# Score banks in a fixed round, VectorE's pair work spread over a slot, and the first pair prepared ahead of a branch, in a fused attention and MLP kernel

## The chip, the cores and the metric

One core of one Trainium2 chip runs the whole program. The metric is device time in microseconds (us) of one execution; smaller is better.

TensorE, VectorE (DVE in the profile), ScalarE (ACT), GpSimd (POOL) and SyncE (SP) work side by side on their own queues. PE is TensorE's matmuls, PEld its weight loads.

## The reference

```python
def rmsnorm(x, g):
    return x / np.sqrt(np.mean(x * x, axis=-1, keepdims=True) + 1e-06) * g
# q, k, v: 8 batches, 12 heads, 448 rows, 64 columns (float32)
q_n, k_n = rmsnorm(q, g_q), rmsnorm(k, g_k)
scores = q_n @ k_n.T / sqrt(64)                  # per batch and head
attn = softmax(scores)                           # (max subtraction cut here)
x = (attn @ v) as rows of 768                    # 3584 rows
h = x @ w_in                                     # 768 by 2048, float64 input
out = (h - np.tanh(h)) @ w_out                   # 2048 by 768, float64 input
```

## The kernel before

The program takes two heads at a time: 8 batches of 6 pairs make 48 steps. It has a software pipeline with one *slot* per step. In slot `s` TensorE computes the scores of pair `s+1`, the sums ("totals") and values of pair `s`, and turns (transposes) the normalised rows of pair `s+2`; between these it runs stretches of the MLP of the batch before, by `run(gap)`. Slots 0 to 5 have attention only, and the first pieces of weights. Slots 6 to 11 carry the MLP of the first batch. From slot 12 on the other batches follow in a regular round; this is the steady stage.

The MLP's weights come as float64 words. They are rounded to float32 once, early: ScalarE (`round_weight_a`, L71 and L72), then VectorE (L78, L79, L82), then GpSimd (L90). Three raw buffers go round, and SyncE refills one when it is free. Most of this falls in slots 6 to 11, inside `run(gap)`.

```python
    ps_s = pool("ps_s", bufs=5, space=PSUM)      # five PSUM banks for attention
    ps_m = pool("ps_m", bufs=3, space=PSUM)      # three for products
    def sc_bank():
        return ps_s.tile([P, 512], F32, name="sc")

    def scores(s, c):                            # 64x448 scores of key block c, both heads
        ...                                      # c == KF: the short last block, "p_last"
        tiles = [sc_bank() for _ in range(2)]    # one bank for each head
        ...                                      # matmuls, then per head:
            nc.scalar.activation(p[...], tiles[h][:, :n], AF.Exp, scale=rr[...])

    def slot(s):
        gap = gap_ns(s)
        if s < 2 * NP:                           # NP = 6 pairs of a batch
            totals(s, sc_bank())                 # ends with VectorE's reciprocal
        if has(s + 1):
            scores(s + 1, 0)
            scores(s + 1, 1)
        ...
        run(gap)                                 # MLP products, weight rounding
        if has(s + 2):
            turn(s + 2, sc_bank(), sc_bank())    # ScalarE copies kT and qT out
        ...                                      # squares(s + 3), loads
        run(gap)
        if has(s + 1):
            scores(s + 1, KF)
        ...
        av = [sc_bank() for _ in range(2)]       # the two values banks
        last_values(s, av)
        ...
        divide(s, values(s, av))                 # VectorE: xT = av * reciprocal
        if has(s + 1):
            scores(s + 1, 2)                     # "the second score" below
            add(s + 1)                           # VectorE: sums of exponentials
        if has(s + 3):
            norm(s + 3)                          # VectorE sums, GpSimd power
        run(gap)
        if has(s + 3):
            norm_q(s + 3)                        # VectorE: query rows times power
        run(gap)
```

Before all this, gain vectors are loaded, a flag is worked out from them (it chooses between a path without a row maximum and a general path), and all loads of `q`, `k`, `v` stand behind the branch on that flag.

## Time and profile before

| kernel before | |
|---|---|
| time, median of 3 runs | 1478.01 us (1473.65 to 1478.78) |
| span of the profiled run | 1474.3 us |
| TensorE busy | 1434.7 us, 97% |
| VectorE busy | 809.9 us, 55% |
| first scores; turn in slot 1 | 13.88 us; 37.20 us |
| a slot of the steady stage | 28.94 us, in some slots more |

TensorE bounds the kernel, and the 97% is an average over three stages. The lines that show them (windows, TensorE's waits, two timelines and the chain of waits) stand in the prediction below. Read there which engine is most loaded in which stage: the DMA engines in the opening (from 10 us on), VectorE in the first batch (slots 6 to 11, about 80 to 320 us), and TensorE alone from 320 us on.

This is ScalarE's timeline of the kernel before in slot 8 (start, length, engine, line, operation, output<-input, and in brackets the idle time before it with who ended it):

```profile
176.49 0.91 ACT L71 ACTIVATE w_out<-w_raw 128x768 f32<-128x768 f32 x1 [5.09 <-DMA w_raw<-in_moe_w_out_dram]
177.31 0.89 ACT L72 ACTIVATE w_raw<-w_raw 128x768 int32<-128x768 uint32 x1
178.09 0.77 ACT L422 ACTIVATE p_last<-sc,rr 128x224 f32<-128x224 f32 x2
```

And this is TensorE at the same place, in the same kernel:

```profile
173.42 1.02 PE L417 MATMUL sc<-qT,kT 64*128 64x448 f32 x2
179.53 1.83 PE L417 MATMUL sc<-qT,kT 64*128 64x448 f32 x2 [5.10 <-DVE xT L498]
```

TensorE waits 5.10 us and the profile names VectorE's division (xT, L498), whose signal came at 179.4. But ScalarE's exponential `p_last`, which frees two other banks of the same five, ended at 178.86, only half a microsecond before. It stood in ScalarE's queue behind a weight piece whose transfer had not landed. Nothing asks for those two banks at this moment, so the late exponential has no wait line.

### The profile page before, as it was taken

To read this page: it belongs to the slowest core of one execution; us is meant where nothing else is said; L and a number is where in the kernel's file an instruction comes from. 1 tells how busy PE (TensorE), PEld (TensorE's weight loads), DVE (VectorE), ACT (ScalarE), POOL (GpSimd) and SP (SyncE) were. 2 spreads that over 40 slices of the span, in tenths; PEclk is the share of its full clock that TensorE was granted. 3 is DMA by queue.
4 is the path that set the end of the run, shared out by engine and by line. 5 is a ranking of instruction groups with operands and counts; after the bars stand their busy time and mean duration, and the time that the engine had idled before them with its cause. 6 is when DMAs were issued, how large, how long until landed. Compare 5 with 4: busy or idle time off the path is not lost.

```text
span 1474.3 us, 26066 instructions
## 1 busy us (share of the span) xinstructions
PE 1434.7 (97%) x10272; PEld 1186.9 (81%) x10272; DVE 809.9 (55%) x1245; ACT 455.3 (31%) x850; POOL 508.5 (34%) x378
## 2 busy tenths in 40 slices
PE   6989899999999999999999999999999999999997
PEld 2558664488888888888888888888888888899997
DVE  3997888755554565347535654555555366433322
ACT  5754553133212332223322233213322233200100
POOL 4655656323331334213422233232333133312310
PEclk9999999999999999999999999999999999999999
DMA  8767787864556544654555555546555654455563
GB/s 177 171 190 201 244 252 204 230 186 148 167 145 175 174 143 144 187 166 149 185 141 169 151 163 162 163 138 182 154 167 142 167 183 135 148 166 157 187 191 97
DMA packets 268055, 250.74 MB, mean 170 GB/s; under 512 B 164884, under 2 KB 210196, under 8 KB 267924
## 3 DMA queue, kind: packets, MB, share of 16 engines
q1 hardware_dynamic: 267600, 248.97, 58.0%
q8 instruction: 84, 1.38, 0.4%
q14 instruction: 47, 0.39, 0.1%
q10 hardware_dynamic: 324, 0.00, 0.0%
HBM read 215.48 MB, written 33.42 MB: 169 GB/s over the span
## 4 chain that ended last, share of the span: by engine, by line
PE 89%; DVE 5%; DMA 2%; SPq 2%; ACT 1%; issue 1%; POOL 0%; ACTq 0%; DVEq 0%; POOLq 0%
PE mm L553 64%; PE sc L417 9%; PE sc L464 6%; PE mm L718 5%; PE sc L485 2%; PE sc L452 1%; PE sc L390 1%; PE sc L394 1%; SPq L182 1%; DVE rs L490 1%; SPq L230 1%; DVE xT L498 1%; PE mm L464 0%; DVE w_out L78 0%; DMA gT<-in_moe_w_in_dram 0%
## 5 line engine op out<-in xcount | busy, mean ns | idle before, releaser
L553 PE MATMUL mm<-xT,w_f 128*128 128x224 f32 x1392 | 280.8, 355 | 4.6 <-DVE s L619 4.6
L553 PEld LDWEIGHTS mm<-xT,w_f 128*128 128x128 f32 x1392 | 259.3, 190 | 25.5 <-issue 9.8
L553 PEld LDWEIGHTS mm<-gT,w_f 128*128 128x128 f32 x1344 | 251.4, 190 | 22.5 <-issue 11.4
L553 PE MATMUL mm<-gT,w_f 128*128 128x224 f32 x1344 | 267.7, 355 | 0.0
L373 POOL TENSOR_TENSOR rr<-rr,neg_half 112x8 f32<-112x8 f32 x96 | 157.9, 1666 | 314.3 <-DVE rr L372 314.2
L553 PE MATMUL mm<-tt,w_f 128*128 128x224 f32 x1044 | 211.2, 354 | 0.0
L553 PEld LDWEIGHTS mm<-tt,w_f 128*128 128x128 f32 x1044 | 196.1, 190 | 7.8 <-issue 7.8
L553 PE MATMUL mm<-tg,w_f 128*128 128x224 f32 x1008 | 200.4, 353 | 0.0
L553 PEld LDWEIGHTS mm<-tg,w_f 128*128 128x128 f32 x1008 | 189.5, 190 | 0.0
L417 PE MATMUL sc<-qT,kT 64*128 64x448 f32 (+1 forms) x960 | 172.9, 498 | 12.8 <-DVE xT L498 7.8
L422 ACT ACTIVATE p<-sc,rr 128x448 f32<-128x448 f32 x192 | 106.1, 637 | 200.2 <-PE sc L417 200.2
L590 POOL TENSOR_TENSOR gT<-s,th 128x448 f32<-128x448 f32 x96 | 112.8, 1182 | 153.6 <-ACT th L589 153.6
L513 POOL TENSOR_TENSOR tt<-xT,tt 128x224 f32<-128x224 f32 x23 | 32.4, 1409 | 335.5 <-DVE xT L498 335.5
L417 PEld LDWEIGHTS sc<-qT,kT 64*128 64x128 f32 (+1 forms) x960 | 62.4, 166 | 82.2 <-issue 70.1
L490 DVE RECIPROCAL rs<-sc 128x224 f32<-128x224 f32 x42 | 65.4, 1557 | 77.6 <-PE sc L485 77.5
L422 ACT ACTIVATE p_full<-sc,rr 128x448 f32<-128x448 f32 x96 | 56.0, 632 | 150.1 <-PE sc L417 150.1
L589 ACT ACTIVATE th<-s 128x448 f32<-128x448 f32 x96 | 55.4, 577 | 120.8 <-DVE s L619 63.4
L672 DVE TENSOR_TENSOR s<-mm,s 128x224 f32<-128x224 f32 x21 | 8.2, 392 | 141.8 <-PE mm L553 141.8
L464 PE MATMUL sc<-p,v_nat 128*32 128x224 f32 x1344 | 79.1, 353 | 0.0
L718 PE MATMUL mm<-gT,w_out 128*128 128x448 f32 x192 | 76.0, 552 | 0.0
L422 ACT ACTIVATE p_last<-sc,rr 128x224 f32<-128x224 f32 x96 | 37.9, 448 | 114.9 <-PE sc L417 114.9
L498 DVE TENSOR_TENSOR xT<-sc,rs 64x224 f32<-64x224 f32 x168 | 65.3, 389 | 9.7 <-PE sc L464 2.3
(118 smaller groups left out, 1623.6 us busy)
## 6 DMA issues: line engine op xcount, KB each, us to landing
w_f<-w_in SPq DMA_DIRECT2D x196, 384.0 KB, 3.4
w_f<-w_out SPq DMA_DIRECT2D x147, 512.0 KB, 3.9
w_raw<-in_moe_w_out_dram SPq DMA_DIRECT2D x16, 768.0 KB, 5.1
q_nat<-in_q_dram SPq DMA_DIRECT2D x48, 224.0 KB, 4.6
out_dram<-th SPq DMA_DIRECT2D x192, 56.0 KB, 2.2
k_nat<-in_k_dram SPq DMA_DIRECT2D x96, 96.0 KB, 3.8
v_nat<-in_v_dram SPq DMA_DIRECT2D x48, 192.0 KB, 3.8
w_in<-w_out SPq DMA_DIRECT2D x21, 384.0 KB, 6.0
```

The source lines that it names most:

```text
L373: nc.gpsimd.tensor_tensor(out=r, in0=r, in1=neg_half[:rows], op=ALU.pow)
L417: nc.tensor.matmul(tiles[h][i * keys : (i + 1) * keys, :n], lhsT=kT[r, c * P : c * P + keys], rhs=qT[r, i * n : (i + 1) * n], start=True, ...
L422: nc.scalar.activation(p[:, h, c if c < 2 else 0, :], tiles[h][:, :n], AF.Exp, scale=rr[:, 0, 2 * c + h : 2 * c + h + 1])
L464: nc.tensor.matmul(av[n][r : r + BL, :HS], lhsT=v_nat[:, h, c, m * BL : (m + 1) * BL], rhs=p[c][:, h, n * HS : (n + 1) * HS], start=False, ...
L485: nc.tensor.matmul(dn[r : r + BL, :HS], lhsT=by[n], rhs=moving[2 * n + h], start=(i == 0), stop=(i == len(parts) - 1),)
L490: nc.vector.reciprocal(rs, dn[:, :HS])
L498: nc.vector.tensor_tensor(out=x[m * D : (m + 1) * D, n * HS : (n + 1) * HS], in0=av[n][m * D : (m + 1) * D, :HS], in1=rs[n * D : (n + 1) * ...
L513: eng.tensor_tensor(out=t2, in0=x22, in1=t1, op=ALU.subtract)
L553: nc.tensor.matmul(bank[:, f * HS : (f + 1) * HS], lhsT=w[:, c * width + f, :], rhs=moving[p](c), start=(first and f == 0 and c == 0), sto ...
L589: nc.scalar.activation(th, h, AF.Tanh, bias=0.0, scale=1.0)
L590: eng.tensor_tensor(out=g[:, rows, cols], in0=h, in1=th, op=ALU.subtract)
L718: nc.tensor.matmul(bank[:, :S], lhsT=w_out_row(f, n // HC)[:, n % HC * P : (n % HC + 1) * P], rhs=g[:, f, :], start=(f == 0), stop=(f == C ...
```

## The change

The intent has three parts. (a) The loads, squares, sums and powers of the first pair go ahead of the branch, so that they need not wait for the flag. (b) The banks are handed out in a fixed round, so that the second score no longer draws a bank that VectorE's division must free. (c) VectorE's work for coming pairs, which stood in one block, is spread over four places of a slot. The diff, cut to its core:

```diff
+    with tc.manual_schedule(), tc.tile_pool(name="g", bufs=1) as gp:   # ahead of the branch
+        nc.scalar.dma_start(out=grow[:, 0, :], in_=g_q[None, :])
+        nc.scalar.dma_start(out=grow[:, 1, :], in_=g_k[None, :])
+        for name, src in (("q", q), ("k", k)):
+            fetch(nc, name, early[name], src[0, 0:2])
+        for i, src in enumerate((g_q, g_k)):
+            nc.sync.dma_start(out=gcol[:, i : i + 1], in_=src[:, None])
+        nc.scalar.activation(warm, warm, AF.Exp)
 ...                                              # constants, flag
+        squares_of(nc, early["sq"], early["n"], early["q"], early["k"])
+        norm_of(nc, early["rr"], early["sq"], early["n"], neg_half)
     bounded = nc.values_load(flag[0:1, 0:1])
 ...
-    ps_s = pool("ps_s", bufs=5, space=PSUM)
-    ps_m = pool("ps_m", bufs=3, space=PSUM)
+    ps = pool("ps", bufs=1, space=PSUM)
+    banks = {name: [ps.tile([P, 512], F32, name=f"{name}{i}") for i in range(n)] for name, n in (("sc", 5), ("mm", 3))}
+    turns = {"sc": 0, "mm": 0}
+    def bank_of(name):
+        turns[name] += 1
+        return banks[name][turns[name] % len(banks[name])]
     def sc_bank():
-        return ps_s.tile([P, 512], F32, name="sc")
+        return bank_of("sc")
 ...
             scores(s + 1, 2)
-            add(s + 1)
-        if has(s + 3):
-            norm(s + 3)
-        run(gap)
-        if has(s + 3):
-            norm_q(s + 3)
-        run(gap)
+        for work, n in ((add, 1), (add_last, 1), (norm, 3), (norm_q, 3)):
+            run(gap / 2)
+            if has(s + n):
+                work(s + n)
```

Cut away: `add` is split in `add` and `add_last`; `sq`, `n`, one sum tile and the first pair's rows become fixed tiles; the gain column is made after the first `norm_q`; the general path has smaller buffers.

More of the change, by code (lines that the diff above doesn't have):

```diff
@@ L90, in round_weight_c, with fetch, squares_of, norm_of @@
     nc.gpsimd.tensor_tensor(out=bits, in0=bits, in1=raw[:, :, 0], op=ALU.add)
-def bounded_path(tc, ctx, q, k, v, moe_w_in, moe_w_out, out, g_col, ident, ones, half_ones, neg_half):
+def fetch(nc, name, t, pair):
+    S = pair.shape[1]
+    P = 128
+    KF, KR = S // P, S % P
+    if name == "q":
+        nc.sync.dma_start(
+            out=t.rearrange("p h c d -> p h (c d)"), in_=pair.rearrange("h (p c) d -> p h (c d)", c=NCH)
+        )
+        return
+    full, rest = pair[:, : KF * P].rearrange("h (p c) d -> h p c d", c=KF), pair[:, KF * P :]
+    if name == "v":
+        last = t[:, :, KF]
+        nc.sync.dma_start(
+            out=t[:, :, :KF].rearrange("p h c d -> p h (c d)"), in_=full.rearrange("h p c d -> p h (c d)")
+        )
+    else:
+        last = t[:, KF]
+        for h in range(2):
+            nc.sync.dma_start(out=t[:, :KF, h], in_=full[h])
+    for r in range(2):
+        nc.sync.dma_start(out=last[r * KR : (r + 1) * KR], in_=rest.rearrange("h p d -> p h d"))
+def squares_of(nc, sq, n, q, k):
+    nc.scalar.activation(n.rearrange("p c h d -> p (c h) d"), q.rearrange("p a b d -> p (a b) d"), AF.Square)
+    nc.scalar.activation(sq, k.rearrange("p a b d -> p (a b) d"), AF.Square)
+def norm_of(nc, rr, sq, n, neg_half):
+    D = sq.shape[2]
+    for i, x in ((1, n.rearrange("p c h d -> p (c h) d")), (0, sq)):
+        rows = x.shape[0]
+        r = rr[:rows, i]
+        nc.vector.reduce_sum(r, x, axis=AX.X)
+        nc.vector.tensor_scalar(out=r, in0=r, scalar1=1.0 / D, scalar2=1e-6, op0=ALU.mult, op1=ALU.add)
+        nc.gpsimd.tensor_tensor(out=r, in0=r, in1=neg_half[:rows], op=ALU.pow)
+def bounded_path(tc, ctx, q, k, v, moe_w_in, moe_w_out, out, g_col, ident, ones, half_ones, neg_half, early):
     nc = tc.nc
@@ L148, in bounded_path @@
     wp = wp_stack.enter_context(tc.tile_pool(name="wp", bufs=1))
-    ps_s = pool("ps_s", bufs=5, space=PSUM)
-    ps_m = pool("ps_m", bufs=3, space=PSUM)
+    ps = pool("ps", bufs=1, space=PSUM)
[4 more added lines that the diff above has]
+        return banks[name][turns[name] % len(banks[name])]
     def mm_bank():
-        return ps_m.tile([P, 512], F32, name="mm")
+        return bank_of("mm")
     loaded = {}
@@ L160, in load @@
             src = {"q": q, "k": k, "v": v}[name]
-            bufs = 3 if name == "v" else 2
-            pair = src[b, 2 * hp : 2 * hp + 2]
-            if name == "q":
-                t = nat.tile([CP, 2, NCH, D], F32, name="q_nat", bufs=bufs)
-                nc.sync.dma_start(
-                    out=t.rearrange("p h c d -> p h (c d)"), in_=pair.rearrange("h (p c) d -> p h (c d)", c=NCH)
-                )
-            else:
-                full, rest = pair[:, :K0].rearrange("h (p c) d -> h p c d", c=KF), pair[:, K0:]
-                if name == "v":
-                    t = nat.tile([P, 2, NCH, D], F32, name="v_nat", bufs=bufs)
-                    last = t[:, :, KF]
-                    nc.sync.dma_start(
-                        out=t[:, :, :KF].rearrange("p h c d -> p h (c d)"), in_=full.rearrange("h p c d -> p h (c d)")
-                    )
-                else:
-                    t = nat.tile([P, NCH, 2, D], F32, name="k_nat", bufs=bufs)
-                    last = t[:, KF]
-                    for h in range(2):
-                        nc.sync.dma_start(out=t[:, :KF, h], in_=full[h])
-                for r in range(2):
-                    nc.sync.dma_start(out=last[r * KR : (r + 1) * KR], in_=rest.rearrange("h p d -> p h d"))
+            if s == 0 and name != "v":
+                t = early[name]
+            else:
+                shape = [CP, 2, NCH, D] if name == "q" else [P, NCH, 2, D] if name == "k" else [P, 2, NCH, D]
+                t = nat.tile(shape, F32, name=f"{name}_nat", bufs=3 if name == "v" else 2)
+                fetch(nc, name, t, src[b, 2 * hp : 2 * hp + 2])
             loaded[name, s] = t
@@ L358, in squares @@
     def squares(s):
-        n = nat.tile([CP, NCH, 2, D], F32, name="n", bufs=1)
-        sq = nat.tile([P, 2 * NCH, D], F32, name="sq", bufs=1), n.rearrange("p c h d -> p (c h) d")
-        normed[s] = sq, n
-        for i, name in ((1, "q"), (0, "k")):
-            nc.scalar.activation(sq[i], loaded[name, s].rearrange("p a b d -> p (a b) d"), AF.Square)
-    def norm(s):
-        sq, n = normed[s]
-        rr = small.tile([P, 2, 2 * NCH], F32, name="rr", bufs=3)
-        for i, rows in ((1, CP), (0, P)):
-            r = rr[:rows, i]
-            nc.vector.reduce_sum(r, sq[i], axis=AX.X)
-            nc.vector.tensor_scalar(out=r, in0=r, scalar1=1.0 / D, scalar2=1e-6, op0=ALU.mult, op1=ALU.add)
-            nc.gpsimd.tensor_tensor(out=r, in0=r, in1=neg_half[:rows], op=ALU.pow)
-        normed[s] = rr, n
+        squares_of(nc, early["sq"], early["n"], loaded["q", s], loaded["k", s])
+    def norm(s):
+        rr = normed[s] = small.tile([P, 2, 2 * NCH], F32, name="rr", bufs=3) if s else early["rr"]
+        if s:
+            norm_of(nc, rr, early["sq"], early["n"], neg_half)
     def norm_q(s):
-        rr, n = normed[s]
+        rr, n = normed[s], early["n"]
         t = loaded.pop(("q", s))
@@ L385, in turn @@
     def turn(s, tk, tq):
-        rr, n = normed.pop(s)
+        rr, n = normed.pop(s), early["n"]
         kn = loaded.pop(("k", s))
@@ L434, in add, with add_last @@
             return
-        t = sp.tile([P, 2, S], F32, name="sum")
+        t = early["sum"]
         sums[s] = [t]
-        p, last = full(s), probs[s, KF][:, :, 0]
+        p = full(s)
         nc.vector.tensor_tensor(out=t, in0=p[0], in1=p[1], op=ALU.add)
         nc.vector.tensor_tensor(out=t, in0=t, in1=p[2], op=ALU.add)
-        for n in range(2):
+    def add_last(s):
+        last = probs[s, KF][:, :, 0]
+        for n in range(2 if sums[s] else 0):
+            t = sums[s][0]
             part = t[n * KR : (n + 1) * KR, :, n * HS : (n + 1) * HS]
@@ L770, in first_slot @@
             load(s + 4, "qk")
-        squares(s + 3)
+        if s > -3:
+            squares(s + 3)
         norm(s + 3)
@@ L785, in first_slot @@
             add(s + 1)
+            add_last(s + 1)
         norm_q(s + 3)
+        if s == -3:
+            early["g_col"]()
         if has(s):
@@ L830, in bounded_path @@
     done[0] = 1
-    warm = small.tile([1, 1], F32, name="warm", bufs=1)
-    nc.vector.memset(warm, 0.0)
-    nc.scalar.activation(warm, warm, AF.Exp)
     for s in range(-3, NP):
@@ L861, in general_path @@
     qkp = ctx.enter_context(tc.tile_pool(name="qkp", bufs=2))
-    ap = ctx.enter_context(tc.tile_pool(name="ap", bufs=5))
+    ap = ctx.enter_context(tc.tile_pool(name="ap", bufs=4))
     atp = ctx.enter_context(tc.tile_pool(name="atp", bufs=3))
@@ L865, in general_path @@
     thp = ctx.enter_context(tc.tile_pool(name="thp", bufs=2))
-    op = ctx.enter_context(tc.tile_pool(name="op", bufs=3))
+    op = ctx.enter_context(tc.tile_pool(name="op", bufs=2))
     ps_s = ctx.enter_context(tc.tile_pool(name="ps_s", bufs=3, space=PSUM))
@@ L878, in load @@
         for name, src in (("k", k), ("q", q), ("v", v)):
-            t = nat.tile([CP, 2, NCH, D], F32, name=f"{name}_nat", bufs=3 if name == "v" else 2)
+            t = nat.tile([CP, 2, NCH, D], F32, name=f"{name}_nat", bufs=2)
             nc.sync.dma_start(
@@ L1092 @@
     consts = ctx.enter_context(tc.tile_pool(name="consts", bufs=1))
-    row_stack = ctx.enter_context(ExitStack())
-    rows = row_stack.enter_context(tc.tile_pool(name="rows", bufs=1))
-    grow = rows.tile([1, 2, D], F32, name="grow")
-    nc.scalar.dma_start(out=grow[:, 0, :], in_=g_q[None, :])
-    nc.scalar.dma_start(out=grow[:, 1, :], in_=g_k[None, :])
-    gcol = consts.tile([P, 2], F32, name="gcol")
-    for base in (0, D):
-        nc.scalar.dma_start(out=gcol[base : base + D, 0:1], in_=g_q[:, None])
-        nc.scalar.dma_start(out=gcol[base : base + D, 1:2], in_=g_k[:, None])
@@ L1102 @@
-    prod = rows.tile([1, D], F32, name="prod")
-    nc.vector.tensor_tensor(out=prod, in0=grow[:, 0, :], in1=grow[:, 1, :], op=ALU.mult)
-    nc.vector.tensor_tensor(out=prod, in0=prod, in1=prod, op=ALU.mult)
+    rows = consts.tile([P, 4 * NCH * D], F32, name="rows")
+    early = {
+        "q": rows[:CP, 2 * NCH * D :].rearrange("p (h c d) -> p h c d", h=2, c=NCH),
+        "k": rows[:, : 2 * NCH * D].rearrange("p (c h d) -> p c h d", c=NCH, h=2),
+        "sum": rows[:, : 2 * S].rearrange("p (h s) -> p h s", h=2),
+        "n": consts.tile([CP, NCH, 2, D], F32, name="n"),
+        "sq": consts.tile([P, 2 * NCH, D], F32, name="sq"),
+        "rr": consts.tile([P, 2, 2 * NCH], F32, name="rr"),
+    }
@@ L1105 @@
+    gcol = consts.tile([D, 2], F32, name="gcol")
     most = consts.tile([1, 1], F32, name="most")
-    nc.vector.tensor_reduce(out=most, in_=prod, op=ALU.max, axis=AX.X)
-    row_stack.close()
     flag = consts.tile([1, 1], I32, name="flag")
-    nc.vector.tensor_scalar(
-        out=flag, in0=most, scalar1=(SCORE_MAX / (scale * D)) ** 2, scalar2=None, op0=ALU.is_le
-    )
+    warm = consts.tile([1, 1], F32, name="warm")
     g_col = consts.tile([P, 1], F32, name="g_col")
-    nc.vector.tensor_scalar(
-        out=g_col, in0=gcol[:, 0:1], scalar1=gcol[:, 1:2], scalar2=scale, op0=ALU.mult, op1=ALU.mult
-    )
@@ L1116 @@
     ident = consts.tile([P, P], F32, name="ident")
-    make_identity(nc, ident)
     ones = consts.tile([P, D // 2], F32, name="ones")
-    nc.vector.memset(ones, 1.0)
     half_ones = consts.tile([P, 2, D // 2], F32, name="half_ones")
-    nc.vector.memset(half_ones, 0.0)
-    for i in range(2):
-        nc.vector.memset(half_ones[i * D : (i + 1) * D, i], 1.0)
     neg_half = consts.tile([P, 2 * NCH], F32, name="neg_half")
-    nc.vector.memset(neg_half, -0.5)
-    bounded = nc.values_load(flag[0:1, 0:1])
+    with tc.manual_schedule(), tc.tile_pool(name="g", bufs=1) as gp:
+        grow = gp.tile([1, 2, D], F32, name="grow")
+        prod = gp.tile([1, D], F32, name="prod")
+        nc.scalar.dma_start(out=grow[:, 0, :], in_=g_q[None, :])
[4 more added lines that the diff above has]
+            nc.sync.dma_start(out=gcol[:, i : i + 1], in_=src[:, None])
+        nc.vector.memset(warm, 0.0)
+        nc.scalar.activation(warm, warm, AF.Exp)
+        make_identity(nc, ident)
+        nc.vector.memset(neg_half, -0.5)
+        nc.vector.memset(ones, 1.0)
+        nc.vector.memset(half_ones, 0.0)
+        for i in range(2):
+            nc.vector.memset(half_ones[i * D : (i + 1) * D, i], 1.0)
+        nc.vector.tensor_tensor(out=prod, in0=grow[:, 0, :], in1=grow[:, 1, :], op=ALU.mult)
+        nc.vector.tensor_tensor(out=prod, in0=prod, in1=prod, op=ALU.mult)
+        nc.vector.tensor_reduce(out=most, in_=prod, op=ALU.max, axis=AX.X)
+        nc.vector.tensor_scalar(
+            out=flag, in0=most, scalar1=(SCORE_MAX / (scale * D)) ** 2, scalar2=None, op0=ALU.is_le
+        )
+        squares_of(nc, early["sq"], early["n"], early["q"], early["k"])
+        norm_of(nc, early["rr"], early["sq"], early["n"], neg_half)
@@ L1128, with make_g_col @@
+    bounded = nc.values_load(flag[0:1, 0:1])
+    def make_g_col():
+        for base in (0, D):
+            nc.vector.tensor_scalar(
+                out=g_col[base : base + D], in0=gcol[:, 0:1], scalar1=gcol[:, 1:2], scalar2=scale,
+                op0=ALU.mult, op1=ALU.mult,
+            )
+    early["g_col"] = make_g_col
     with tc.If(bounded) as cmp:
         with ExitStack() as arm, tc.manual_schedule():
-            bounded_path(tc, arm, q, k, v, moe_w_in, moe_w_out, out, g_col, ident, ones, half_ones, neg_half)
+            bounded_path(tc, arm, q, k, v, moe_w_in, moe_w_out, out, g_col, ident, ones, half_ones, neg_half, early)
@@ L1131 @@
     with cmp.Else():
         with ExitStack() as arm:
+            make_g_col()
             general_path(tc, arm, q, k, v, moe_w_in, moe_w_out, out, g_col, ident, neg_half)
```

## The prediction

> **What bounds the kernel now.** I read the page's busy shares first: TensorE is busy 97% of 1474.3 us, so at most 39.6 us of idle time can be won, plus whatever its matmuls lose to a lower clock. Then I cut the span into windows, to see where that loss lies (columns: stretch, length, busy time and instructions of TensorE, its weight loads, VectorE, ScalarE and GpSimd, granted clock, DMA share, GB/s).
>
> ```profile
> 20.00:30.00 10.00, 9.49 (x95) 4.59 (x98) 4.29 (x8) 9.38 (x18) 5.32 (x3) 1.00 1.04 229
> 80.00:120.00 40.00, 37.31 (x310) 26.80 (x302) 34.52 (x51) 18.76 (x31) 20.86 (x13) 0.89 0.74 220
> 160.00:200.00 40.00, 34.90 (x237) 27.34 (x236) 34.18 (x44) 19.01 (x30) 22.23 (x13) 0.91 0.75 227
> 400.00:600.00 200.00, 199.29 (x1419) 172.07 (x1412) 104.31 (x166) 56.49 (x110) 64.44 (x50) 1.00 0.54 159
> ```
>
> There are three stages. Up to 40 us the DMA engines are full (share 0.93 to 1.04). From 40 to 320 us weights are rounded while the first batch is worked: VectorE is busy 85%, TensorE has holes, and the clock falls below 1. From 320 us TensorE is all but always busy, so there only a wait of TensorE itself counts. Its waits over the whole span (who waited, for whom, us in total, times, longest):
>
> ```profile
> PE mm L390 <- DMA k_nat<-in_k_dram: 8.0, 1, 8.0
> PE sc L417 <- DVE xT L498: 7.8, 2, 5.1
> PE mm L553 <- DVE s L619: 4.6, 6, 1.1
> PE sc L394 <- DVE n L379: 3.0, 1, 3.0
> PE mm L390 <- DVE rs L490: 2.7, 2, 2.5
> ```
>
> The 7.8 us are two waits of a score matmul, at 106.9 and 174.4 us. TensorE's timeline at the first, then the windows after it:
>
> ```profile
> 105.86 1.02 PE L417 MATMUL sc<-qT,kT 64*128 64x448 f32 x2
> 109.53 1.71 PE L417 MATMUL sc<-qT,kT 64*128 64x448 f32 x2 [2.66 <-DVE xT L498]
> ...
> 110.00:112.00 2.00, 2.00 (x4) 0.79 (x3) 1.84 (x5) 0.64 (x1) 1.42 (x2) 0.50 1.22 229
> 112.00:116.00 4.00, 4.00 (x12) 3.60 (x12) 0.62 (x1) 2.15 (x3) 3.58 (x3) 0.50 0.90 227
> ```
>
> Two of the four matmuls of one score pair wait 2.66 us, and then the clock is 0.50 for over 6 us: the hole costs more than its own length. The 4.6 us are six waits at a regular place of the steady stage, seen in the chain of waits (start, length, what):
>
> ```profile
> 488.41 5.51 PE mm L553 x28
> 493.92 0.02 issue
> 493.94 0.64 DVE s L619
> 494.58 0.04 issue
> 494.62 5.56 PE mm L553 x28
> ```
>
> There VectorE has `add` (sum, 488.60 to 492.2) and `norm` (492.23 to 493.9) in one block, and the eviction L619, which frees the bank TensorE wants, queues behind it. For the opening, the DMA issues of SyncE (start, length):
>
> ```profile
> 4.10 0.39 SPq L165 DMA_DIRECT2D q_nat<-in_q_dram  x1
> ...
> 7.24 0.60 SPq L165 DMA_DIRECT2D q_nat<-in_q_dram  x1
> ...
> 10.48 2.01 SPq L230 DMA_DIRECT2D gT<-in_moe_w_in_dram  x4
> ```
>
> SyncE does nothing before 4.10, because the first load stands behind the branch on the flag; then it issues without a pause to 17.75.
>
> **What the Trainium skill says.** "TensorE: Matmul & The Clock Gate", Part 1, says that the array drops to half clock after about 3.4 us idle and needs about as long a busy stretch to recover. The trace agrees on the halving (0.50 above) and shows it after the hole of 2.66 us[...]. "SBUF — State Buffer", "SBUF: two separate sides", says that VectorE with two SBUF inputs and GpSimd exclude each other for a whole instruction. The trace agrees: the query normalisation L379 takes 0.69 us alone, and 4.06 us at 671.03, where three GpSimd subtractions L590 of 3.32 us run. "DMA: Bandwidth & Descriptors", "Issuing engines are not separate DMA queues", says that all queues share the 16 DMA engines; so an early start wins only what those engines have free, 0.34 of them busy in the first 10 us. "ScalarE: Activation LUTs", "What ACT_TABLE_LOAD costs", gives 1283 ns for a table load; the trace has 1.28 us, at 6.72 us, late because its dummy input waits behind the last gain vector.
>
> **The change part by part.**
> (a) Opening. First pair's loads, squares, sums and power go ahead of the branch, the table load too. SyncE can start at about 0.74, when ScalarE issues its first DMA now. Five issues take 3.1 us (4.10 to 7.20), then two issues for the gain columns of some 0.6 us each (those on ScalarE took 0.5 to 0.6), then the flag and the branch, 0.64 us (3.46 to 4.10): 0.74 + 3.1 + 1.2 + 0.64 = 5.7. So the second pair's loads start at 5.7 in place of 7.24, 1.5 us earlier, though the first pair's are 3.4 earlier. The compute chain gains more: key rows land about 4.7 (now 8.0), first scores about 9 (now 13.88). But the chain then runs through SyncE's queue and the DMA engines (waits of 5.30, 6.43 and 5.85 us on loads at 12.6, 21.7 and 28.2), which are full from 10 to 40 us; it moves by the transfers' head start, 1.5 to 3.4. I take 2.0.
> (b) Banks. The compiled program of the kernel before lists the bank of each tile. The pool hands banks out by when they come free, not in turn: in the slots 6, 7 and 8 the two value banks are 2 and 0, and the second score bank right after is again 2. So that score waits for VectorE's division L498, which queues behind weight rounding. That is the 2.66 and the 5.1 us (in slot 7 VectorE is not late). In a fixed round of five, a slot of 13 draws takes 0; 1 2 3 4; 0 1; 2 3; 4 0; 1 2: the last two scores get banks whose readers are ScalarE's (a qT or kT copy and an exponential), done by then. Both waits go. Gross: slot 6, 2.66 idle, 1.2 on the two matmuls (1.71 for 0.51) and 2.6 on the next 56 products (13.39 in place of 10.79): 6.5 us. Slot 8, 5.1 + 1.3 + 1.7 (12.48 for 10.79) = 8.1 us. Together 14.6. VectorE's work stays: 169 us busy in the 200 from 80 to 280. In 185 us it would be 91%, so part returns as short waits for weights or evictions. I keep 60%: 9 us. The three product banks went in a fixed round already; nothing there.
> (c) VectorE's work spread. `add`, `add_last`, `norm` and `norm_q` go to four places half a gap (14 products, 2.7 us) apart. No block exceeds add's 2.4 us, against the 24 products, 4.6 us, that pass between a bank's last product and its next use. By the chain, a slot takes 28.94 us; five slots of the later batches take 0.96 more (the L619 wait and its tail), six others 0.23 more (L611, the same block), and the first one at 319.7 some 1.1: 4.8 + 1.4 + 1.1 = 7.3. Norm_q now follows norm by 2.7 us where the pair of powers takes 3.2, so it may block VectorE a little. I take 6.5.
> (d) One sum tile and one row tile kept outside the pools, and the other arm's smaller buffers: nothing on the path.
> Sum: 2.0 + 9 + 6.5 = 17.5. 1478.0 less 17.5 is 1460.5; I predict 1461.
>
> **The rivals.**
> First, VectorE becomes the bound of the first batch: the two holes are not caused by the bank but by VectorE's lateness, and TensorE stops a little later at the next eviction or weight. For: VectorE is without a gap from 157.6 to 208.7, and GpSimd stretches its rounding (L79 0.98 us mean, 0.56 when alone). Against: in 112 to 132 it waits some 7 us for TensorE. Then (b) is worth 2 to 4 and the time is about 1467.
> Second, the opening is hidden: the weights behind the loads fill the DMA engines anyway, or SyncE's extra issues eat the head start. Then (a) is 0 and the time about 1463. The opposite, that the whole 3.4 or 4.9 us passes through, gives 1458 to 1460.
> Third, the late norm_q meets GpSimd's subtractions at a slot's end, holds VectorE up to 4 us, and a new wait for an eviction takes the place of the L619 one, in some slots. Then (c) is 2 to 3 in place of 6.5: about 1465.
> All three at once leave some 1473; all favourable, some 1453.
>
> **Range and chances.** The three runs spread by 5 us, so 1452 to 1471 should hold it 8 times in 10. Two per cent is 29.6 us. The idle 39.6 us include about 8 at the end (last store) and 5 of unavoidable opening, and the lost clock is some 10; to win 29.6, nearly every hole would have to close. Faster by over 2%: 0.05. Slower: nothing is added to the path, 0.01. Within 2%: 0.94.
>
> **What would show it.** In the profile after: SyncE's first q issue near 0.7 and its second near 5.7; the first scores near 9; the turn at 37.2 now about 35. No wait of L417 on the division, and the clock in 80 to 120 and 160 to 200 us near 1.0 in place of 0.89 and 0.91. No wait of L553 on the eviction after product 3, and TensorE's slot pitch 28.94 in all slots. If the L417 waits vanish but waits of L553 or L718 on VectorE or GpSimd appear in 110 to 250 us, rival one holds. I would be wrong outright if the steady pitch itself moved, or if the fixed round brought TensorE new waits on ScalarE.

## The result, and the profile after

| | before | after |
|---|---|---|
| time, median of 4 runs of the same job | 1477.26 us (1473.65 to 1478.78) | 1464.64 us (1462.88 to 1465.69) |
| ratio, 95% interval | 1 | 0.9917 (0.9895 to 0.9939) |
| span of the profiled run | 1474.3 us | 1463.9 us |
| TensorE busy | 1434.7 us | 1429.9 us |

A ratio here is the mean time of one kernel's runs over that of the kernel before's runs of the same rounds, so not quite the ratio of the medians quoted. Where microseconds are given for a ratio, they are (1 - ratio) times 1476: here 12.3 us, 0.8%. All outputs are right.

The four stages of the profile after, in the columns that the prediction explains:

```profile
20.00:30.00 10.00, 10.00 (x112) 5.42 (x112) 4.30 (x8) 7.75 (x15) 5.32 (x3) 0.79 1.07 222
80.00:120.00 40.00, 39.35 (x356) 29.78 (x349) 39.07 (x55) 22.58 (x37) 22.79 (x14) 1.00 0.72 222
160.00:200.00 40.00, 31.61 (x204) 21.98 (x202) 33.01 (x39) 18.46 (x29) 21.06 (x13) 0.85 0.75 231
400.00:600.00 200.00, 200.00 (x1472) 171.79 (x1471) 102.43 (x165) 55.99 (x110) 63.12 (x49) 1.00 0.58 165
```

From 80 to 120 us TensorE's busy time rose from 37.31 to 39.35 and the clock from 0.89 to 1.00; from 400 to 600 us it is busy throughout. In the opening (20 to 30 us) the clock fell from 1.00 to 0.79. But from 160 to 200 us it is *worse* than before: 31.61 busy in place of 34.90, clock 0.85 in place of 0.91. TensorE's waits after (who waited, for whom, us in total, times, longest):

```profile
PE sc L438 <- ACT p_last L443: 9.2, 3, 6.1
PE mm L411 <- DVE rr L129: 5.0, 1, 5.0
PE sc L438 <- ACT p L443: 3.1, 1, 3.1
PE mm L411 <- DVE rs L515: 2.7, 2, 2.6
PE sc L415 <- DVE g_col L1164: 2.5, 1, 2.5
PE sc L411 <- DVE rs L515: 2.3, 1, 2.3
PE mm L578 <- DVE s L634: 0.6, 1, 0.6
```

The wait on the division is gone, and so is the regular wait for an eviction. Two new ones stand in slots 8 and 9: 6.1 us for ScalarE's `p_last`, and 2.3 us of a transpose for VectorE's reciprocal (rs). TensorE's timeline after, at the places in slots 6, 8 and 9:

```profile
104.22 1.02 PE L438 MATMUL sc<-qT,kT 64*128 64x448 f32 x4
105.17 2.16 PE L578 MATMUL mm<-xT,w_out 128*128 128x224 f32 x10
...
164.66 1.02 PE L438 MATMUL sc<-qT,kT 64*128 64x448 f32 x2
171.79 1.86 PE L438 MATMUL sc<-qT,kT 64*128 64x448 f32 x2 [6.12 <-ACT p_last L443]
...
198.33 1.12 PE L411 MATMUL sc<-ident,k_nat 128*128 128x128 f32 x4 [2.28 <-DVE rs L515]
```

In slot 6 the four score matmuls now run in one piece, followed at once by products. In slot 8 the same pair of matmuls stops for 6.12 us. ScalarE's timeline of the kernel after says why:

```profile
163.90 0.94 ACT L72 ACTIVATE w_raw<-w_raw 128x768 int32<-128x768 uint32 x1
169.70 0.91 ACT L71 ACTIVATE w_out<-w_raw 128x768 f32<-128x768 f32 x1 [4.87 <-DMA w_raw<-in_moe_w_out_dram]
170.52 0.89 ACT L72 ACTIVATE w_raw<-w_raw 128x768 int32<-128x768 uint32 x1
171.31 0.76 ACT L443 ACTIVATE p_last<-sc,rr 128x224 f32<-128x224 f32 x2
```

It is the pattern of the kernel before: the exponential stands behind a weight piece that waits for its transfer. Only now a score needs its bank. Why the transfer was late stands in the queues of GpSimd and SyncE:

```profile
162.58 2.47 POOL L90 TENSOR_TENSOR w_out<-w_out,w_raw 128x768 int32<-128x768 int32 x1 [1.54 <-PE sc L438]
165.08 5.14 SPq L265 DMA_DIRECT2D w_raw<-in_moe_w_out_dram  x2
```

GpSimd's rounding frees a raw buffer at 165.05; SyncE issues the transfer at 165.08, and ScalarE starts on the piece at 169.70, 4.6 us later. GpSimd's L90 in turn stands right behind VectorE's L82 (161.49 to 162.45). So a late VectorE reaches this exponential in a ring: VectorE's rounding, GpSimd's rounding, the raw buffer, the transfer, ScalarE. VectorE's timeline of the kernel after, at the starts of slots 8 and 9:

```profile
148.88 2.33 DVE L400 TENSOR_TENSOR n<-q_nat,rr 112x512 f32<-112x512 f32 x1
151.14 1.54 DVE L515 RECIPROCAL rs<-sc 128x224 f32<-128x224 f32 x1
...
194.79 2.02 DVE L400 TENSOR_TENSOR n<-q_nat,rr 112x512 f32<-112x512 f32 x1
196.73 1.54 DVE L515 RECIPROCAL rs<-sc 128x224 f32<-128x224 f32 x1
```

The query normalisation (L400, `norm_q`), 0.69 us when alone, takes 2.33 and 2.02 us. At the first place GpSimd's rounding L90 runs from 148.23 to 150.67, across most of it. In its new place `norm_q` is the last work of a slot, so it stands right ahead of the next slot's reciprocal, which frees the totals' bank; and in the fixed round that very bank is the first one that the turn draws.

In the steady stage, the chain of waits after is TensorE alone (start, length, what):

```profile
484.12 10.79 PE mm L578 x56
494.91 1.71 PE sc L438 x8
496.62 5.49 PE mm L578 x28
```

At last, SyncE's issues in the opening after (SPq is its queue):

```profile
0.74 0.38 SPq L99 DMA_DIRECT2D rows<-in_q_dram  x1
...
6.05 0.33 SPq L99 DMA_DIRECT2D q_nat<-in_q_dram  x1
...
9.05 2.01 SPq L261 DMA_DIRECT2D gT<-in_moe_w_in_dram  x4
```

To see where time comes from and where it goes, take the start of the key transposes in each slot, from TensorE's timeline of each kernel's one profile, and subtract that of the kernel before:

| transposes in slot | before, us | after | banks alone | spread alone | opening alone | late spread | p_last early |
|---|---|---|---|---|---|---|---|
| 1 | 37.20 | -1.66 | -0.09 | +0.80 | +0.62 | -1.61 | -1.92 |
| 6 | 95.84 | -2.25 | -0.19 | +0.75 | -0.14 | -1.76 | -2.34 |
| 7 | 133.32 | -8.60 | -6.18 | +0.76 | -0.17 | -7.64 | -8.89 |
| 8 | 163.70 | -8.76 | -6.34 | +1.34 | -0.17 | -7.80 | -8.82 |
| 9 | 203.24 | -4.91 | -7.06 | +3.75 | -0.48 | -8.52 | -12.02 |
| 10 | 235.18 | -3.24 | -7.05 | +5.79 | -0.47 | -8.29 | -11.73 |
| 12 | 302.03 | -2.66 | -7.21 | +3.96 | -0.25 | -8.12 | -15.56 |
| 13 | 332.34 | -4.03 | -7.57 | +2.59 | -0.63 | -9.49 | -16.93 |
| 45 | 1264.66 | -10.28 | -7.56 | -3.65 | -0.63 | -15.74 | -23.18 |

Read a column downwards: a step between two rows is won or lost in the slots between. The column "after" wins 6.35 us in slot 6, gives 3.85 back in slot 8 and 1.67 in slot 9, and wins 6.25 in the steady stage. The other columns are experiments told next (the last two are `late_again` and `kf_early`). Each is one profile. Kernels that do not touch the opening differ from before by up to 0.8 us in slot 1, and by 2.0 in slot 2 in `no_opening` below, so a small step up to there says little. The gain from slot 13 to slot 45, in contrast, is 6.24 or 6.25 us in every profile that has the spread.

The profiled run of the changed kernel was its slowest. Its second profile, `changed_again` below, gives back 3.2 us in slots 8 and 9 (from -8.92 to -5.76 in slot 10) where this one gives back 5.5, though the two waits are as long (5.93 and 2.29 us beside 6.12 and 2.28). What differs is the clock after them: 0.78 from 176 to 180 us and 0.79 from 200 to 204 in this profile, 0.97 and 1.00 in the second.

### The profile page after: what moved, and what is told of

Read it like the earlier page. It is cut to its first block, busy times and chain, and to the rows that moved or that the text cites. A ratio compares the mean times of both kernels' runs of the same rounds, so it can differ in the third digit from the quotient of the medians.

```text
span 1463.9 us, 26034 instructions
## 1 busy us (share of the span) xinstructions
PE 1429.9 (98%) x10272; PEld 1187.1 (81%) x10272; DVE 818.6 (56%) x1246; ACT 456.7 (31%) x850; POOL 512.0 (35%) x378
## 4 chain that ended last, share of the span: by engine, by line
PE 89%; DVE 5%; DMA 2%; SPq 1%; ACT 1%; issue 1%; POOL 0%; ACTq 0%
PE mm L578 64%; PE sc L438 9%; PE sc L489 6%; PE mm L743 4%; PE sc L477 1%; PE sc L510 1%; PE sc L411 1%; PE sc L415 1%; DMA q_nat<-in_q_dram 1%; DVE w_out L82 1%; DVE rs L515 1%; DVE w_out L78 1%; DMA gT<-in_moe_w_in_dram 1%; DVE w_out L79 1%; DVE w_out L320 1%
## 5 line engine op out<-in xcount | busy, mean ns | idle before, releaser
L615 POOL TENSOR_TENSOR gT<-s,th 128x448 f32<-128x448 f32 x96 | 121.2, 1267 | 297.3 <-ACT th L614 296.6
L438 PE MATMUL sc<-qT,kT 64*128 64x448 f32 (+1 forms) x960 | 172.6, 503 | 12.9 <-ACT p_last L443 9.2
```

Source lines behind the costliest of these rows:

```text
L438: nc.tensor.matmul(tiles[h][i * keys : (i + 1) * keys, :n], lhsT=kT[r, c * P : c * P + keys], rhs=qT[r, i * n : (i + 1) * n], start=True, ...
L615: eng.tensor_tensor(out=g[:, rows, cols], in0=h, in1=th, op=ALU.subtract)
```

## The experiments

Three jobs, four kernels each, each timed against the kernel before (1475.65, 1474.84 and 1476.45 us, medians).

My theory after the result: the fixed round does its work in slot 6, but in slot 8 it exchanges the division's wait for that of `p_last`; and the spread is worth its size in the steady stage but costs in the first batch, since its late `norm_q` delays the reciprocal there. The rival: VectorE is the bound of the first batch, and the lost time would appear there whatever the bank or the order.

### Each part alone

`banks_only` is the kernel before with the bank lines of the diff; `spread_only` is the kernel before with `add` split and the loop of four places; `opening_only` has the new opening with the old pools and the old order.

> The kernel before with the fixed round of banks alone. My theory now: the wait of the score in slot 6 goes and its 6.4 us with it, but in slot 8 the second score bank is then one that ScalarE's exponential p_last must free, and p_last stands behind a weight piece that waits for its transfer; so a wait of 4 to 6 us on p_last stays there and most of the gain is lost by slot 9. Expected 1 to 5 us faster than before. The prediction's size (9 us, both waits gone) would make it 8 to 10 us faster. The six L619 waits of the steady stage must still be there in both.

Measured: 1468.43 us, ratio 0.9952 (0.9936 to 0.9968), 7.1 us. The second score in slot 8 and TensorE's waits in this kernel:

```profile
167.07 1.02 PE L423 MATMUL sc<-qT,kT 64*128 64x448 f32 x2
172.25 1.86 PE L423 MATMUL sc<-qT,kT 64*128 64x448 f32 x2 [4.16 <-ACT p_last L428]
```

```profile
PE sc L423 <- ACT p_last L428: 7.4, 4, 4.2
PE mm L559 <- DVE s L625: 4.5, 7, 0.8
```

The 7.1 us lie between what the two sides expected. The wait for `p_last` needs neither the spread nor the opening: the fixed round itself brings it. Slot 6 gives 6.0 us (from -0.19 to -6.18), slot 8 only 0.7. The eviction wait of the steady stage is still there, 4.5 us, as it must be without the spread.

> The kernel before with VectorE's work in a slot spread, nothing else. My theory: the waits on the eviction after product 3 go, every later slot takes 28.94 us, 6 to 8 us faster than before; the two score waits on the division (2.7 and 5.1 us) stay, perhaps 1 us longer. Rival (late norm_q meets GpSimd): only 2 to 3 us faster, with new waits of TensorE at slot ends.

Measured: 1471.25 us, ratio 0.9968 (0.9953 to 0.9984), 4.7 us. The wait for the division in this kernel, in place of 5.1 us as the longest before:

```profile
PE sc L417 <- DVE xT L502: 9.7, 2, 7.0
```

The column "spread alone" loses 2.4 us in slot 8 and 2.0 in slot 9, gets 1.8 back later, and wins 7.6 from slot 12 on (from +3.96 to -3.65). By the total alone this is a miss for both sides, since it lies between them. By stages it is plain: the spread does what was worked out for it where TensorE bounds, and costs where VectorE queues.

> The changed kernel with banks from the pools and VectorE's work in its old blocks, so the early opening alone. My theory: the fourth turn comes 1.7 us sooner, as SyncE's second pair of loads is only 1.2 us sooner and the DMA engines are full to 40 us; the whole is 1 to 2.5 us faster than before. Rivals: nothing (hidden behind the weight loads), or the full 3.0 to 3.7 us of the first scores.

Measured: 1473.96 us, ratio 0.9989 (0.9973 to 1.0004), 1.6 us, not clear of zero. Its profile had no lead left by slot 1 and next to none in slot 6. The trace shows where it went: TensorE waited 2.39 us for `p_last` at 32.15 us, and then the clock was 0.50 from 35 to 40 us, where it is 1.00 in the changed kernel. The opening by itself does not explain this. From 32 to 42 us the clock is 0.66 or 0.83 in five of the fourteen profiles, two of them without the opening (`spread_only`, `no_opening`), and 1.00 in the other nine. Of these nine, the seven with the opening are 1.4 to 1.9 us ahead of the kernel before at the transposes of slot 5, and `banks_only` is 0.1 ahead.

### One part taken out

`no_banks`, `no_spread` and `no_opening` are the changed kernel without one part each (`no_opening` was built from the other side, as the kernel before with the banks and the spread); `changed_again` is the changed kernel itself, run again in the third job.

> The changed kernel with banks from the pools: opening and spread. If parts add, 1.6 + 4.7 = 6.3 us faster than before, about 1469, with both waits on the division back (about 2.7 us in slot 6, 7 us in slot 8).

> The changed kernel with VectorE's work in its old blocks: banks and early opening together. If the parts add, it is 7.1 + 1.6 = 8 to 9 us faster than before, about 1467, with the six waits on the eviction after product 3 back, and slot 8's wait on p_last about 4 us rather than 6.1. If the changed kernel's wait of 6.1 us in slot 8 comes from the banks and not from the spread, it stays at 6.

> The kernel before with banks and spread, without the early opening. If the opening is worth its 1.6 us alone, this is 1 to 2 us slower than the changed kernel. If banks and spread only add, 7.1 + 4.7 = 11.8 us faster than before; if the spread takes more where the banks have won (both meet in slot 8), 9 to 11.

> The changed kernel itself, to stand beside the next three on one chip. 11 to 13 us faster than before; in slot 8 a wait of about 6 us on p_last, in slot 9 one of about 2.3 us on the reciprocal.

Measured, with the parts alone, in us won over the kernel before:

| parts in the kernel | ratio (95%) | us won |
|---|---|---|
| opening | 0.9989 (0.9973 to 1.0004) | 1.6 |
| spread | 0.9968 (0.9953 to 0.9984) | 4.7 |
| banks | 0.9952 (0.9936 to 0.9968) | 7.1 |
| opening, spread (`no_banks`, 1469.70 us) | 0.9962 (0.9945 to 0.9979) | 5.6 |
| banks, opening (`no_spread`, 1467.44 us) | 0.9955 (0.9942 to 0.9969) | 6.6 |
| banks, spread (`no_opening`, 1464.54 us) | 0.9925 (0.9910 to 0.9941) | 11.1 |
| all (`changed_again`, 1463.27 us) | 0.9913 (0.9898 to 0.9929) | 12.8 |

Banks and spread add up within the error (7.1 + 4.7 = 11.8 beside 11.1). The opening adds 0.9 to the spread, 1.7 to both, and takes 0.5 from the banks: about 1 us, and with intervals of some 2 us to either side it is not told from zero nor from its predicted 2.

The traces of these kernels also split the wait of slot 8. The longest wait for `p_last` is 4.2 us with the banks alone and 4.0 in `no_spread`, but 6.0 in `no_opening`, which has banks and spread. With the banks of the pools it is the wait for the division that grows, from 5.1 (`opening_only`) to 7.0 (`no_banks`). So some 4 us of the 6.1 come with the banks and 2 with the spread.

### `p_last` early

`kf_early` puts the scores of the last key block, and with them `p_last`, ahead of the weight pieces in ScalarE's queue, in slots 6 to 11 only. Nothing but these scores and exponentials moves; the banks are drawn in the same order.

```diff
+        if s < 2 * NP and has(s + 1):
+            scores(s + 1, KF)
         run(gap)
-        if has(s + 1):
+        if s >= 2 * NP and has(s + 1):
             scores(s + 1, KF)
```

> The changed kernel, but in the slots 6 to 11 the scores of the last keys and their exponential p_last are emitted ahead of the second stretch of products, so ahead of the weight pieces in ScalarE's queue. Theory: p_last behind a weight piece is the only cause of the waits of 6.1 us in slot 8 and 2.1 us in slot 10; both go, and 5 to 10 us with them against the changed kernel, about 1457. Rival: VectorE and the weight chain are the bound of the first batch; the waits move to an eviction or a weight, and the gain is under 2 us.

Measured: 1454.61 us, ratio 0.9860 (0.9842 to 0.9879), 20.7 us: the changed kernel and 8 us more. ScalarE in slot 8 now:

```profile
159.12 0.78 ACT L443 ACTIVATE p_last<-sc,rr 128x224 f32<-128x224 f32 x2
...
169.42 0.92 ACT L71 ACTIVATE w_out<-w_raw 128x768 f32<-128x768 f32 x1 [5.02 <-DMA w_raw<-in_moe_w_out_dram]
```

The weight piece waits as long as ever for its transfer (5.02 us), but `p_last` is done ten microseconds before. TensorE's four score matmuls run in one piece at 164.78. This is what remains of its waits for evictions and for `p_last` (the second one lies in the opening, at 33 us; in slots 6 to 11 three more, for GpSimd and the reciprocal, make 1.2 us together):

```profile
PE mm L578 <- DVE s L636: 2.0, 1, 2.0
PE sc L438 <- ACT p_last L443: 0.7, 1, 0.7
```

So the 6.1 us were ScalarE's order. VectorE has the same rounding to do as in the changed kernel, and TensorE goes 12.9 us ahead of it by slot 13 (10.0 if `changed_again` is taken); that speaks against VectorE as the bound. What is left of the rival is the one wait of 2.0 us, a product for an eviction (L636) that stands behind rounding and the division. It is not small: slot 8 now gives 3.2 us (from -8.82 to -12.02), not the 8.1 of the prediction. The window view of this kernel around it shows what a hole of that size costs:

```profile
168.00:172.00 4.00, 4.00 (x22) 3.70 (x20) 3.93 (x5) 2.58 (x4) 1.78 (x1) 1.00 0.54 104
172.00:174.00 2.00, 0.05 (x1) 0.00 (x0) 1.88 (x6) 0.62 (x2) 1.84 (x1) 1.00 0.75 250
174.00:176.00 2.00, 1.95 (x6) 1.81 (x7) 1.93 (x4) 0.63 (x1) 0.00 (x0) 0.60 1.03 415
176.00:178.00 2.00, 2.00 (x7) 1.82 (x7) 2.00 (x3) 1.09 (x2) 1.19 (x1) 0.54 1.06 423
178.00:180.00 2.00, 2.00 (x12) 2.00 (x11) 1.93 (x3) 0.00 (x0) 0.65 (x1) 1.00 1.01 399
```

TensorE is busy to 172 us, idle for 2, and then gets about half the clock for most of 4 us: 13 matmuls in 4 us, where the next 2 us take 12.

### The spread from slot 12 on only

`spread_late` keeps the old order in slots 6 to 11, where weights are rounded, and has everything else of the change. `late_again` is the same kernel in the third job, beside the changed kernel.

```diff
+        if s < 2 * NP:
+            add(s + 1); add_last(s + 1); norm(s + 3)     # (three lines, put in one here)
+            run(gap)
+            norm_q(s + 3)
+            run(gap)
+            return
         for work, n in ((add, 1), (add_last, 1), (norm, 3), (norm_q, 3)):
```

> The changed kernel, but in the slots 6 to 11 the sum, norm and norm_q stand where they stood before (norm right after the division, norm_q one stretch later); the spread begins at slot 12. The runs of single parts showed that the spread alone loses some 4 us between the turns of slots 7 and 9 and wins 7.6 later. Theory: norm_q, just ahead of the reciprocal at a slot's start and held 2 us by a GpSimd rounding step, makes VectorE late there; without it the changed kernel gains 3 to 4 us, to about 1461. Rival: VectorE's lateness is the weights' own, the loss stays, gain under 1 us.

> The changed kernel with the spread only from slot 12, again, now beside the changed kernel. If the spread's loss in the slots 8 and 9 is real and not one of profiles alone, 2 to 5 us faster than the changed kernel; rival: within 1 us of it.

Measured: 1460.59 us, ratio 0.9903 (0.9887 to 0.9918), and again 1460.22 us, ratio 0.9893 (0.9876 to 0.9909). In the third job its runs (1460.04 to 1460.71) all lie below those of the changed kernel (1461.12 to 1466.11); the medians differ by 3.05 us. TensorE's waits of the two, first the changed kernel again, then the late spread:

```profile
PE sc L438 <- ACT p_last L443: 8.8, 3, 5.9
PE sc L411 <- DVE rs L515: 2.3, 1, 2.3
```

```profile
PE sc L438 <- ACT p_last L443: 7.0, 3, 4.0
```

The wait for the reciprocal in slot 9 is gone and the one for `p_last` is 4.0, as with the banks alone (4.2). Some 3 us of the spread's gain had been given back in the first batch. This is the loss that my theory put there, and slots 6 to 11 are the only place where the two kernels differ.

### Both mends

`two_mends` joins the two edits.

> The changed kernel with both: p_last ahead of the weight pieces in slots 6 to 11 (this alone won 10 us) and the spread from slot 12 only. Theory of two separate losses: the second adds 1 to 3 us to the 10, about 1452. Rival (one loss, seen twice, since both end in the same wait of slot 8): the same as with p_last alone, 1453 to 1456.

Measured: 1452.99 us, ratio 0.9849 (0.9836 to 0.9863), the fastest kernel, 22.3 us below the kernel before. Over `kf_early` (another job) that is 1.6 us, inside the intervals, and in the traces the two stand level in slot 45 (-23.21 and -23.18). So the two losses look for the most part like one; the times alone fit both sides of what was expected. The late `norm_q` costs by way of the wait for `p_last`: in the third job that wait ended at 171.44 us in the changed kernel and at 170.60 with the late spread, though it began 1.1 us later there. The ring shown above carries it: with the late spread the reciprocal began 1.14 us sooner (149.84 for 150.98), the rounding L82 0.80, the transfer's issue 0.81 and `p_last` 0.84. Once `p_last` is early, the late `norm_q` costs little.

### The gain columns on another queue

`gcol_act` issues the two gain columns from ScalarE, so that SyncE reaches the second pair's loads sooner.

```diff
-            nc.sync.dma_start(out=gcol[:, i : i + 1], in_=src[:, None])
+            nc.scalar.dma_start(out=gcol[:, i : i + 1], in_=src[:, None])
```

> The changed kernel with the two gain-column loads issued by ScalarE's queue in place of SyncE's. Theory that SyncE's issues bound the opening: its second pair starts 1.2 us sooner and the fourth turn comes 1 to 1.3 us sooner, of which up to 1.2 us reach the end. Rival, the DMA engines bound it: the fourth turn moves by less than 0.4 us and the time is the same.

Measured: 1460.78 us, ratio 0.9904 (0.9889 to 0.9919), beside 0.9917 and 0.9913 for the changed kernel: within the error. Its issues:

```profile
4.77 0.33 SPq L99 DMA_DIRECT2D q_nat<-in_q_dram  x1
```

The second pair's loads go out 1.28 us sooner than in the changed kernel (6.05), yet the transposes in slot 1 came only 0.31 us sooner (35.23 beside 35.54), which is within the scatter. SyncE's issue time did not bound the opening here; this agrees with DMA engines that are full (share 1.07 from 20 to 30 us).

## Why the prediction was right, and where it was off

The time (1464.6 us beside 1461, range 1452 to 1471) and the "within 2%" hold. The two terms that carry it were each some 2 us too large, and the steps show which part.

**What bounds it, and the three stages: right.** Gains and losses fell where the stages said: 6.35 us in slot 6, 6.25 + 1.37 us from slot 12 on, 1.4 to 1.9 by slot 5 from the opening where no half clock disturbed it.

**(a) Opening, predicted 2.0: mechanism right, size not resolved.** SyncE's first issue at 0.74 and second q load at 6.05 (predicted 5.7), first scores at 10.21 (predicted about 9), the turn of slot 1 at 35.54 (predicted about 35). Of a head start of 3.67 us in the first scores, 1.66 was left in slot 1. The times give it about 1 us, with zero inside the error; the undisturbed profiles have 1.4 to 1.9 in slot 5, close to what was predicted. The kernel with the opening alone lost its lead to a wait and a half clock that also struck kernels without the opening.

**(b) Banks, predicted 9: measured 7.1.** The gross sum was 6.5 for slot 6 and 8.1 for slot 8. Slot 6 came as worked out: 6.0 in `banks_only`, 6.35 in the changed kernel. Slot 8 gave 0.7 in `banks_only`. The step that failed is "the last two scores get banks whose readers are ScalarE's (a qT or kT copy and an exponential), done by then". The banks were as said; the exponential was not done by then, since ScalarE's queue held it behind a weight piece waiting for its transfer. The profile of before had shown it (176.49 to 178.86 above), but only in ScalarE's timeline: the wait line named the division, which ended half a microsecond later, and nothing waited for the banks of the exponential. The factor of 60% was put there for VectorE; it came out near 50% (7.1 of 14.6) for another reason. That the term lies near its number is therefore luck: the discount was right in size and meant for another engine.

**(c) Spread, predicted 6.5: measured 4.7 alone.** In the steady stage the sum of 7.3 was right: 7.6 in the trace, and every slot there 28.94 us. The term left out is the first batch, where the same loop runs: it lost 2.4 us in slot 8 and 2.0 in slot 9 by itself. The prediction asked about the late `norm_q` in the steady stage alone.

**The rivals.** The first (VectorE becomes the bound) fell in the form given: putting `p_last` ahead won 8 us with VectorE's work unchanged; one wait of 2.0 us on an eviction is what it left. (One reading set down for it was wrong: VectorE is not without a gap from 157.6 to 208.7 us, it stood idle for 2.76 us up to 184.67 and 2.40 up to 187.70. Its 85% hold for 80 to 280 us, 169 of 200; from 40 to 320 it is 82%.) But its outcome, a hole that goes on under another name, came true through ScalarE. The second (opening hidden) stays possible by the times, about 1 us with an error of some 2, though not up to slot 5. The third had the right mechanism, a late `norm_q` held by GpSimd (2.33 and 2.02 us for 0.69), at the wrong place: not at an eviction of the steady stage but ahead of the reciprocal in slots 8 and 9. Its instruction that takes the blame there is GpSimd's rounding, not the subtractions. The last sentence of the prediction had "if the fixed round brought TensorE new waits on ScalarE" among what would make it wrong; that is the one that happened, and it cost the term of slot 8.

**The sum.** 2.0 + 9 + 6.5 = 17.5 was expected; 12.3 to 12.8 came. Slot 8's transfer-bound exponential and the spread's loss in slots 8 and 9 more than cover the gap: mending both gave 22.3.

**Open.** How much of the opening's lead in slot 5 reaches the end; what would shorten the ring that keeps ScalarE waiting 3.2 to 5.4 us for the weight piece of slot 8 in every profile; and why a half clock follows some holes and not others of the same length, as in the two profiles of the changed kernel, which for that reason end 2.9 us apart (-10.28 and -13.20 us in slot 45).

## What to carry to other kernels

When a wait for a buffer is removed by giving its user another buffer, look up when that other buffer's last reader ends *in the present trace*; wait lines say nothing of a buffer that nobody asks for yet. In a queue that works in order, as ScalarE's did here, put the short instruction that frees a shared buffer ahead of work that waits for a transfer, as `kf_early` did for 8 us by moving two lines. A reordering that helps the stage where one engine bounds can cost in another stage where a different queue holds things up: restrict it to the stages it was reasoned for, and check each stage apart.

## What the Trainium skill lacked or had wrong

- "TensorE: Matmul & The Clock Gate", Part 1, "What's actually happening", puts the drop to half clock after at least one idle window of about 3.4 us. Here a hole of 2.00 us (`kf_early`, 172 to 174 us, TensorE busy before it) was followed by a clock of 0.60 and 0.54 for 4 us, and one of 2.66 us in the kernel before by 0.50 for over 6 us. So a half clock came here after holes shorter than the page's. It did not come after every such hole: one of 2.29 us (`changed_again`, up to 197.4 us) was followed by a clock of 1.00.
- "SBUF — State Buffer", "SBUF: two separate sides", says that VectorE with two SBUF inputs and GpSimd exclude each other for the whole instruction. L400 at 2.33 us under a rounding of GpSimd that ran from 148.23 to 150.67 agrees. But in the kernel before the same operation (L379) took 0.63 us at 45.75, more than 0.5 us after the start of one of GpSimd's power instructions on 8 columns (two SBUF inputs, 45.23 to 46.86), and 0.68 at 350.81 under another that ran from 349.86 to 351.73. So not every GpSimd instruction shuts VectorE out to its end, and the page does not say which do not.
- No page has, as far as I read, that a profile's waits say nothing of a reader whose buffer nobody asks for yet. Here such a reader, `p_last`, ended 0.5 us before the one that was named, and of a term of 8.1 us only 0.7 came.
